# Weight-decode steps and three instruction positions in a spectral layer with two experts

## Chip, core and metric

One core of one Trainium2 chip. The number is the device time of one execution in microseconds; a kernel's time is the median of its runs. TensorE is PE in the profile, with PEld for its weight loads; VectorE is DVE, ScalarE is ACT, GpSimd is POOL, SyncE is SP (here it only issues DMAs).

## What is computed

x is 2 x 3008 x 256, float32. The two experts' weight matrices (256 x 2048 in, 2048 x 256 out) come as float64.

```python
X = np.fft.rfft(x, axis=1)
Yr = Xr @ w_r - Xi @ w_i + b_r
Yi = Xr @ w_i + Xi @ w_r + b_i
Yr, Yi = (np.sign(Y) * np.maximum(np.abs(Y) - 0.01, 0.0) for Y in (Yr, Yi))
x = np.fft.irfft(Yr + 1j * Yi, n=3008, axis=1).reshape(6016, 256)
h = x @ moe_w_in;  x = (h - np.tanh(h)) @ moe_w_out
h = x @ moe2_w_in; out = (h * np.clip(h + 3.0, 0.0, 6.0) / 6.0) @ moe2_w_out
```

## The kernel before

**Precision.** Most products take three matmuls (`three_pass`, L118 to L121): each float32 operand is split into a rounded "hi" part (a copy on ACT into the type fp32r) and a "lo" rest (a subtraction on DVE, sometimes on POOL), and hi x hi, hi x lo and lo x hi are summed.

**Spectral part.** The Fourier transform is split as 47 x 64. `dft_a` (47 points) runs for 8 chunks of the first sequence ahead of the loop and for the 8 chunks of the second inside it, one per iteration for t = 0 to 7; its results are stored to DRAM. The loop over t = 0 to 23 (L659 to L717) takes two frequencies per iteration and is pipelined over four stages: `linear(t)` (24 matmuls), `dft_c(t-2)` (6), `dft_b(t+2)` (8), and `dft_a` (4). `load_bi` brings the stored chunks back, `load_bm` and `load_cm` the transform matrices (`bmt` for `dft_b`). Behind `linear(t)` come on DVE the three instructions of `shrink` (L342 to L344: bias and threshold), then `evict_b_lo` (L315), then `shrink_lo` (L354); on ACT `evict_c` (L372), `evict_b_hi` (L308, L309), `shrink_hi` (L350), `evict_b_neg` (L320). From t = 17 on, `dft_d` and `op_hi`, `op_lo`, `op_sub` make the operands of the first expert pass: sums and differences of input blocks, each split into hi and lo; `op_sub` of T3 and T4 is at L716 and L717, on POOL.

**Experts.** 16 passes k (`NS = 8` per expert) of 2 x 376 tokens, each of 8 groups g of 256 hidden columns. A group (`group`, L563) forms its 2 x 2 block product with seven products instead of eight (p1, p2, p5, p6, p3, p7, p4), applies the nonlinearity `nl`, splits the result (`nl_split`), and, between its products, issues the output products `outp` of the group before it. p1, p6, p7 and p4 of a group go through one PSUM bank `al`: p6 waits for ACT's copy of p1 (L575), p7 for ACT's copy of p6 (L587), p4 for DVE's sum with p7 (L596). The very first group (`first_group`, L532) is a generator whose pieces the loop's end places between the last `dft_c`; its copies of p1, p5 and p6 are L538, L540 and L546, its sums L539, L547 and L552.

**Weight decode.** There is no float64 arithmetic: each of 32 chunks (8 each of 1i and 1o for the first expert, then 8 of 2i, 8 of 2o) is loaded as raw 64-bit words (`w_load`, L156, 512 KB), turned into float32 by bit operations and split. `w_steps` (L162) is a generator; one `w_step()` issues one to three instructions. A chunk of an input matrix takes seven steps, one of an output matrix five: the two ACT conversions (L172, L173); DVE's L175 with ACT's hi copy of the chunk before (L182); DVE's L185, behind which SP is given the next raw load; DVE's lo part of the chunk before (L190); the rounding add (L197); and for input matrices two steps of two short adds (L201 to L205). Three raw buffers exist, so the load issued behind L185 has to wait on SP until that L185 is done, and everything later on SP waits with it. Second-expert chunks are stored to DRAM (`w2id`, `w2od`) and reloaded in passes 7 and 8.

The engines' orders are written out by hand (`manual_schedule`): every engine executes its instructions in the order in which the program issues them. Where decode steps go is said by these lines:

```python
NDEC, NST = 13, 2                                  # L138
for _ in range(2):                                 # L679, and range(NST) at L702
    if t > 1 and ptr["dec"] < NDEC:
        w_step()
if 1 <= g < 6 or k == 0 and g > 0:                 # L770
    if (pos in "bcd" or k == 0) and k < NS:
        w_step()
```

`ptr["dec"]` counts finished chunks; `hook` calls `super_hook` at positions a to e of each group: a comes behind the nonlinearity of p1, b behind p3, c and d around the last output products, e at the group's end. With L785 the first pass also makes sure that a group's weights are decoded before it (it finds them so).

Of the kernel before, what the change touches and what calls it, by code (L numbers as in the profile page):

```python
# [87 lines left out]
def spectral_moe_kernel(ctx: ExitStack, tc: tile.TileContext, x, w_r, w_i, b_r, b_i,  # L88
                        w1i, w1o, w2i, w2o, am, bm, cm, dm, out):
    nc = tc.nc  # L90
    pe, act, dve, pool, sp = nc.tensor, nc.scalar, nc.vector, nc.gpsimd, nc.sync
# [43 lines left out]
        W[nm, c] = pl.tile([128, 2, n], F32R, tag=f"w{kind}{c}", name=f"w{kind}{c}")  # L135
        return W[nm, c]

    NDEC, NST = 13, 2  # L138
    w_src = {"1i": w1i, "1o": w1o, "2i": w2i, "2o": w2o}
    w_order = [(nm, c) for c in range(8) for nm in ("1i", "1o")]  # L140
    w_order += [(nm, c) for nm in ("2i", "2o") for c in range(8)]
# [1 line left out]
    ptr = {"load": 0, "dec": 0}  # L143
# [68 lines left out]
    def w_step():  # L212
        next(w_gen, None)
# [98 lines left out]
    def evict_b_lo(j):  # L312
        pq, h = xf_t[j]
        l = wl.tile([128, 4, 192], F32R, tag="fl", name="fl")
        dve.tensor_tensor(out=l[:, :, 64:192], in0=pq, in1=h.bitcast(F32)[:, :, 64:192], op=ALU.subtract)  # L315
        xf_t[j] = (h, l)
# [5 lines left out]
    def linear(j):  # L322
        h, l = xf_t.pop(j)
        p = bank("acc")
        pv = p.rearrange("p (k d) -> p k d", k=2)
        for k in range(2):
            n = 0
            for dh in range(2):
                q = 2 * k + dh
                for wsel, off in ((0, 64), (1, 0)):  # L330
                    three_pass(pv[:, k, :], h[:, q, off:off + 128], l[:, q, off:off + 128],
                               lwH[:, wsel, dh, :], lwL[:, wsel, dh, :], n == 0, n == 3)
                    n += 1
        s_t[j] = pv
# [13 lines left out]
    def shrink_hi(j):  # L348
        s, sh, sl = s_t[j]
        act.activation(out=sh, in_=s, func=ACTF.Copy)  # L350
# [6 lines left out]
    def dft_c(j):  # L357
        b, kp = divmod(j, K1 // 2)
        sh, sl = s_t.pop(j)
        p = bank("acc")  # L360
        pv = p.rearrange("p (k d) -> p k d", k=2)
        for k in range(2):
            kk = 2 * kp + k
            ch, cl = (v[:, kk * 128:(kk + 1) * 128] for v in (cmH, cmL))
            three_pass(pv[:, k, :], ch, cl, sh[:, k, :], sl[:, k, :], True, True)
        s_t[j] = pv
# [10 lines left out]
    NS = 8  # L377
    xtf = bmt.rearrange("p k f -> p (k f)")[:, 0:4 * NT].rearrange("p (a t) -> p a t", a=4)
    ttf = bmt.rearrange("p k f -> p (k f)")[:, 1536:1536 + 4 * NT].rearrange("p (a t) -> p a t", a=4)
    B11, B12, B21, B22 = (xtf[:, i, :] for i in range(4))  # L380
    T1, T2, T3, T4 = (ttf[:, i, :] for i in range(4))
# [24 lines left out]
    def op_sub(out, a, b, eng=pool):  # L406
        eng.tensor_tensor(out=out, in0=a, in1=b, op=ALU.subtract)  # L407
# [200 lines left out]
    with tc.manual_schedule():  # L608
# [19 lines left out]
        for w in (w_r, w_i):  # L628
            t = wl.tile([128, 2, D], F32, tag="ly", name="lwf")
# [27 lines left out]
        NP = K1  # L657
        a_next = 8
        for t in range(NP):  # L659
            linear(t)  # L660
            if t > 1:
                dft_c(t - 2)
            if t + 2 < NP:
                dft_b(t + 2)
            ab = dft_a(a_next, False) if a_next < 16 else None
            if t > 1:
                evict_c(t - 2)
            if t + 2 < NP:
                evict_b_hi(t + 2)
            shrink(t)  # L670
            shrink_hi(t)
            if t + 2 < NP:
                evict_b_lo(t + 2)
            if t == NP - 1:
                first = first_group()
                next(first)
            if t + 2 < NP:
                evict_b_neg(t + 2)
            for _ in range(2):  # L679
                if t > 1 and ptr["dec"] < NDEC:  # L680
                    w_step()
            shrink_lo(t)
            for nm in {20: ("b11", "b21"), 21: ("t1",), 22: ("t2", "b22")}.get(t, ()):
                op_lo(0, nm)
            if t == 20:
                op_sub(T1, B12, B11, dve)
            if t == 21:
                op_sub(T2, B22, T1, dve)
            if ab:
                dft_a_out(a_next, ab)  # L690
                a_next += 1
            flush_stores()
            if t % 2 == 0:
                load_bm(t // 2 + 2)
                load_cm(t // 2 + 1, s_t[t][0].bitcast(F32)[0:1, 0, 0:1])
            if t > 0:
                load_x(10 + t)
            if t in (0, 1):
                w_load()
            if t % 2 == 1:  # L700
                load_bi((t + 1) // 2 + 2)
            for _ in range(NST):  # L702
                if t > 1 and ptr["dec"] < NDEC:
                    w_step()
            if t == 14:
                load_din(0, din0)
            if t == 15:
                load_din(1, x1[2])
            if t in (17, 18):
                dft_d(0, t - 17, "h")  # L710
            if t in (19, 20):
                dft_d(1, t - 19, "h")
            for nm in {19: ("b11", "b21"), 20: ("t1",), 21: ("t2", "b22")}.get(t, ()):
                op_hi(0, nm)
            if t == 22:
                op_sub(T3, B22, B12)  # L716
                op_sub(T4, B21, T2)  # L717

        next(first)
        dft_c(NP - 2)  # L720
# [12 lines left out]
        def super_hook(k, g, pos):  # L733
# [12 lines left out]
            if n < 2 * NS:  # L746
# [20 lines left out]
                    op_sub(T4, B21, T2)  # L767
                if g == 7 and pos == "e":
                    op_split(n, "b22")
            if 1 <= g < 6 or k == 0 and g > 0:  # L770
                if (pos in "bcd" or k == 0) and k < NS:
                    w_step()
            if pos == "e" and k in (NS - 1, NS):
                if k == NS - 1:
                    w_until(17 + g)
# [52 lines left out]
```

## Time and profile before

| | |
|---|---|
| three runs, median (lowest to highest) | 1226.78 us (1226.3 to 1228.44) |
| the profiled execution | 1225.78 us, of which its span is 1224.0 us |
| PE busy | 1183.5 us, 97% |
| PEld busy | 1163.0 us, 95% |
| DVE busy | 962.5 us, 79% |
| ACT busy | 880.8 us, 72% |
| POOL busy | 158.7 us, 13% |
| DMA | 96.51 MB, 79 GB/s over the span |

The page divides the span into 40 slices; PE is at 90% or more in most of them, below that in the first three, the sixth and the eighth. A share of the whole span says little about one stretch, so the rows below are by stretch. A matmul's row gives its start, its duration and how many were merged; matmuls overlap, so a stretch is measured from start to start.

### The profile page before, as it was taken

What the parts mean: (1) busy time and instruction counts of PE and PEld (TensorE: products, weight loads), DVE (VectorE), ACT (ScalarE), POOL (GpSimd) and SP (SyncE); (2) the same over time, 40 slices, a digit from 0 to 9 for tenths busy, and PEclk for the clock granted to TensorE, in tenths of its full rate; (3) what the DMA queues carried; (4) which work ended last, traced back from release to release, by engine and by line L of the source; (5) the groups of instructions that cost most, each with busy time, mean ns of one, the idle gap of its engine ahead of it and who ended that gap; (6) DMA issues with size and microseconds to landing.
All of it is one profiled execution on the core that took longest, in us unless ns stands there. A gap on an engine that the chain in (4) does not pass through costs nothing.

```text
span 1224.0 us, 20880 instructions
## 1 busy us (share of the span) xinstructions
PE 1183.5 (97%) x7824; PEld 1163.0 (95%) x7824; DVE 962.5 (79%) x1808; ACT 880.8 (72%) x1836; POOL 158.7 (13%) x164
## 2 busy tenths in 40 slices
PE   5899979899999999999999999999999999999998
PEld 3799969899999999999999999999999999999998
DVE  0479988888888888888778787878787878787875
ACT  3477767777787777777777777777777777777775
POOL 1000010201102020202021320202020202020200
PEclk9899989999999999999999999999999999999999
DMA  9896522232212122211104530101010101001000
GB/s 269 239 334 209 185 86 67 99 106 74 74 49 98 66 69 69 61 60 44 43 1 166 185 130 1 51 1 52 1 52 1 52 1 35 18 22 31 10 18 26
DMA packets 47797, 96.51 MB, mean 79 GB/s; under 512 B 4448, under 2 KB 27488, under 8 KB 47696
## 3 DMA queue, kind: packets, MB, share of 16 engines
q1 hardware_dynamic: 41728, 74.08, 18.8%
q0 software_dynamic: 4032, 14.68, 3.9%
q10 hardware_dynamic: 1936, 6.42, 1.4%
q8 instruction: 61, 1.00, 0.3%
q14 instruction: 40, 0.33, 0.1%
HBM read 58.73 MB, written 36.44 MB: 78 GB/s over the span
## 4 chain that ended last, share of the span: by engine, by line
PE 76%; DVE 10%; ACT 10%; issue 3%; DMA 2%; SPq 0%; ACTq 0%; DVEq 0%
PE acc L119 13%; PE acc L121 13%; PE acc L120 13%; PE al L119 7%; PE al L120 6%; PE al L121 6%; PE be L121 3%; PE be L120 3%; PE be L119 3%; ACT gh L115 2%; DVE g L440 2%; PE ga L398 2%; PE ga L120 2%; PE ga L121 2%; PE ga L119 1%
## 5 line engine op out<-in xcount | busy, mean ns | idle before, releaser
L116 DVE TENSOR_TENSOR gl<-g,gh 128x376 fp32r<-128x376 f32 x509 | 290.4, 571 | 149.7 <-ACT gh L115 122.1
L115 ACT ACTIVATE gh<-g 128x376 fp32r<-128x376 f32 x509 | 263.5, 518 | 185.5 <-DVE g L443 91.8
L121 PE MATMUL acc<-wo,gl 128*128 128x256 f32 (+1 forms) x768 | 215.9, 281 | 0.0
L120 PE MATMUL acc<-wo,gh 128*128 128x256 f32 (+1 forms) x768 | 215.8, 281 | 0.0
L119 PE MATMUL acc<-wo,gh 128*128 128x256 f32 (+1 forms) x768 | 215.7, 281 | 0.0
L119 PE MATMUL acc<-gh,wo 128*128 128x376 f32 x512 | 173.2, 338 | 0.0
L121 PE MATMUL acc<-gh,wo 128*128 128x376 f32 x512 | 171.0, 334 | 0.0
L120 PE MATMUL acc<-gl,wo 128*128 128x376 f32 x512 | 170.7, 333 | 0.0
L120 PEld LDWEIGHTS acc<-wo,gh 128*128 128x128 f32 (+1 forms) x768 | 143.0, 186 | 0.0
L121 PEld LDWEIGHTS acc<-wo,gl 128*128 128x128 f32 (+1 forms) x768 | 143.0, 186 | 0.0
L119 PEld LDWEIGHTS acc<-wo,gh 128*128 128x128 f32 (+1 forms) x768 | 142.8, 186 | 0.0
L407 POOL TENSOR_TENSOR bmt<-bmt 128x376 f32<-128x376 f32 x62 | 73.9, 1192 | 521.5 <-ACT bmt L400 396.8
L443 DVE SCALAR_TENSOR_TENSOR g<-e,c 128x376 f32<-128x376 f32 x192 | 119.3, 621 | 12.5 <-ACT e L442 7.9
L442 ACT ACTIVATE e<-c,three 128x376 f32<-128x376 f32 x192 | 116.7, 608 | 8.0 <-DVE c L589 7.2
L440 DVE TENSOR_TENSOR g<-c,e 128x376 f32<-128x376 f32 x189 | 113.9, 603 | 8.2 <-ACT e L439 6.0
L423 POOL TENSOR_TENSOR cmL<-bmt,cmH 128x376 fp32r<-128x376 f32 x60 | 66.1, 1102 | 325.8 <-ACT cmH L418 322.5
L439 ACT ACTIVATE e<-c 128x376 f32<-128x376 f32 x189 | 97.5, 516 | 7.9 <-DVE c L589 7.7
L119 PEld LDWEIGHTS acc<-gh,wo 128*128 128x128 f32 x512 | 96.4, 188 | 0.0
L120 PEld LDWEIGHTS acc<-gl,wo 128*128 128x128 f32 x512 | 96.3, 188 | 0.0
L121 PEld LDWEIGHTS acc<-gh,wo 128*128 128x128 f32 x512 | 96.1, 188 | 0.0
L119 PE MATMUL al<-cmH,wi 128*128 128x376 f32 x256 | 87.8, 343 | 6.3 <-ACT bi_all L538 2.9
L579 ACT ACTIVATE s<-be 128x376 f32<-128x376 f32 x127 | 61.9, 487 | 39.8 <-PE be L121 39.4
(164 smaller groups left out, 2830.8 us busy)
## 6 DMA issues: line engine op xcount, KB each, us to landing
raw<-in_moe_w_in_dram SPq DMA_DIRECT2D x16, 512.0 KB, 5.0
raw<-in_moe_w_out_dram SPq DMA_DIRECT2D x16, 512.0 KB, 4.4
w2id<-wout SPq DMA_DIRECT2D x8, 896.0 KB, 4.3
wi<-w2id POOLq DMA_DIRECT2D x8, 896.0 KB, 4.9
bi_all<-s SPq DMA_DIRECT2D x12, 512.0 KB, 6.5
y1d<-y SPq DMA_DIRECT2D x32, 188.0 KB, 2.0
bmt<-y1d SPq DMA_DIRECT2D x8, 752.0 KB, 4.9
s<-co SPq DMA_DIRECT2D x23, 256.0 KB, 5.5
```

Source lines behind the costliest of these rows:

```text
L115: act.activation(out=hi, in_=src, func=ACTF.Copy)
L116: (lo_eng or dve).tensor_tensor(out=lo, in0=src, in1=hi.bitcast(F32), op=ALU.subtract)
L119: pe.matmul(out=out_ap, lhsT=lh, rhs=rh, start=start, stop=False, **kw)
L120: pe.matmul(out=out_ap, lhsT=lh, rhs=rl, start=False, stop=False, **kw)
L121: pe.matmul(out=out_ap, lhsT=ll, rhs=rh, start=False, stop=stop, **kw)
L407: eng.tensor_tensor(out=out, in0=a, in1=b, op=ALU.subtract)
L423: (eng or dve).tensor_tensor(out=l, in0=OPS[nm][0], in1=h.bitcast(F32), op=ALU.subtract)
L439: act.activation(out=e, in_=src, func=ACTF.Tanh)
L440: dve.tensor_tensor(out=g, in0=src, in1=e, op=ALU.subtract)
L442: act.activation(out=e, in_=src, func=ACTF.Relu, bias=three)
L443: dve.scalar_tensor_tensor(out=g, in0=e, scalar=6.0, in1=src, op0=ALU.min, op1=ALU.mult)
L579: act.activation(out=s5, in_=be, func=ACTF.Copy)
```

## The change

The number of decode steps per loop iteration becomes 6 for t < 10 (three at each place), and 2 plus 1 + t % 2 from t = 10 (it was 4 throughout, from t = 2). The loop decodes the same 13 chunks, in 81 steps: t = 2 to 9 issue 48 of them (32 before), the last stands in t = 19 (t = 22 before). In the experts' first pass steps stand at positions a to d of groups 1 to 5 until 16 chunks are done (17 steps); before, at a to e of groups 1 to 7 (35 steps). The 18 others go to passes 1 to 6, which get position a of groups 1, 3 and 5 beside b, c, d of groups 1 to 5. In the last iteration `shrink_hi` comes behind the first piece of `first_group`. T3 and T4 are subtracted on DVE instead of POOL.

```diff
@@ -135,7 +135,7 @@
-    NDEC, NST = 13, 2
+    NDEC = 13
@@ -668,15 +668,17 @@
             shrink(t)
-            shrink_hi(t)
+            if t < NP - 1:
+                shrink_hi(t)
             if t + 2 < NP:
                 evict_b_lo(t + 2)
             if t == NP - 1:
                 first = first_group()
                 next(first)
+                shrink_hi(t)
             if t + 2 < NP:
                 evict_b_neg(t + 2)
-            for _ in range(2):
+            for _ in range(3 if t < 10 else 2):
                 if t > 1 and ptr["dec"] < NDEC:
                     w_step()
@@ -699,7 +701,7 @@
-            for _ in range(NST):
+            for _ in range(3 if t < 10 else 1 + t % 2):
                 if t > 1 and ptr["dec"] < NDEC:
                     w_step()
@@ -713,8 +715,8 @@
             if t == 22:
-                op_sub(T3, B22, B12)
-                op_sub(T4, B21, T2)
+                op_sub(T3, B22, B12, dve)
+                op_sub(T4, B21, T2, dve)
@@ -767,9 +769,10 @@
-            if 1 <= g < 6 or k == 0 and g > 0:
-                if (pos in "bcd" or k == 0) and k < NS:
-                    w_step()
+            if 1 <= g < 6 and k < NS:
+                if pos in "bcd" or pos == "a" and (k == 0 or g % 2):
+                    if k or ptr["dec"] < 16:
+                        w_step()
```

SP's queue in the loop, iterations t = 3 (its end) to t = 5, before. `raw` is a raw weight load, `s_0` a store of `dft_c`'s result, `bmt` a transform table, `xb` a chunk of x, `bi_all` a reload for `dft_b`:

```order
L254 DMA xb_100<-in_x_dram 14x1024
L290 DMA bi_all<-s_0_60 128x4x256
L156 DMA raw<-in_moe_w_in_dram 128x2x256
L259 DMA s_0_62<-co 128x2x256
L613 DMA bmt<-in_bm_dram 128x512
L254 DMA xb_98<-in_x_dram 80x1024
L254 DMA xb_98<-in_x_dram 14x1024
L156 DMA raw<-in_moe_w_out_dram 128x2x256
```

And the same place in the changed kernel:

```order
L290 DMA bi_all<-s_0_60 128x4x256
L156 DMA raw<-in_moe_w_out_dram 128x2x256
L259 DMA s_0_62<-co 128x2x256
L613 DMA bmt<-in_bm_dram 128x512
L254 DMA xb_98<-in_x_dram 80x1024
L254 DMA xb_98<-in_x_dram 14x1024
L156 DMA raw<-in_moe_w_in_dram 128x2x256
```

The raw load of iteration 3 has gone ahead of `xb_100` and `bi_all`, and the `bmt` load of iteration 4 now stands behind a raw load of its own iteration; the same holds in iteration 6.

ACT at the end of the loop (from the last `evict_b_neg`) and in the first pieces of `first_group`, before:

```order
L320 ACTIVATE fl<-fl 128x4x64
L172 ACTIVATE ws<-raw 128x512
L173 ACTIVATE ws<-raw 128x512
L182 ACTIVATE wi_1763<-ws 128x896
L418 ACTIVATE cmH<-bmt 128x376
L418 ACTIVATE b22h<-bmt 128x376
L372 ACTIVATE co<-acc 128x512
L350 ACTIVATE sh<-ly 128x512
L372 ACTIVATE co<-acc 128x512
L350 ACTIVATE sh<-ly 128x512
L538 ACTIVATE bi_all<-al 128x376
L540 ACTIVATE bi_all<-be 128x376
```

And in the changed kernel:

```order
L320 ACTIVATE fl<-fl 128x4x64
L418 ACTIVATE cmH<-bmt 128x376
L418 ACTIVATE b22h<-bmt 128x376
L372 ACTIVATE co<-acc 128x512
L350 ACTIVATE sh<-ly 128x512
L372 ACTIVATE co<-acc 128x512
L538 ACTIVATE bi_all<-al 128x376
L540 ACTIVATE bi_all<-be 128x376
L350 ACTIVATE sh<-ly 128x512
```

The three decode instructions are gone from there, and L538 and L540 stand ahead of the last L350.

DVE in group 7 of the first pass, from its L577 on, before:

```order
L116 TENSOR_TENSOR gl<-g,gh 128x376
L440 TENSOR_TENSOR g<-c_2616,e 128x376
L190 TENSOR_TENSOR wout<-ws,wout 128x896
L589 TENSOR_TENSOR c_2647<-be,su 128x376
L116 TENSOR_TENSOR gl<-g,gh 128x376
L197 ISA ws<-ws 128x1024
L440 TENSOR_TENSOR g<-c_2647,e 128x376
L596 TENSOR_TENSOR c_2670<-al,s_2618 128x376
```

And in the changed kernel:

```order
L116 TENSOR_TENSOR gl<-g,gh 128x376
L440 TENSOR_TENSOR g<-c_2586,e 128x376
L589 TENSOR_TENSOR c_2615<-be,su 128x376
L116 TENSOR_TENSOR gl<-g,gh 128x376
L440 TENSOR_TENSOR g<-c_2615,e 128x376
L596 TENSOR_TENSOR c_2637<-al,s_2588 128x376
```

Only the group's own instructions are left there.

## Rows read from the trace of the kernel before

**Rows 1.** Busy time by stretch: bounds, length, busy us (instructions) by engine, PE clock, DMA.
```profile
42.00:159.60 117.60, 116.08 (x929) 111.80 (x927) 100.91 (x182) 82.92 (x163) 7.80 (x16) 1.00 0.71 227
159.60:180.10 20.50, 13.17 (x65) 11.66 (x64) 17.68 (x34) 11.50 (x24) 1.05 (x1) 0.83 0.32 101
180.10:256.40 76.30, 69.63 (x395) 66.50 (x394) 66.41 (x131) 56.77 (x121) 11.40 (x9) 0.98 0.27 83
256.40:1224.00 967.60, 961.42 (x6340) 954.85 (x6339) 774.76 (x1459) 715.64 (x1504) 134.15 (x128) 1.00 0.16 52
```

**Rows 2.** Who PE waited for, 42 to 180 us: total, times, longest.
```profile
PE al L119 <- ACT bi_all L538: 2.9, 1, 2.9
PE acc L121 <- DVE fl L315: 2.0, 2, 1.5
...
PE al L119 <- DVE bi_all L552: 0.7, 1, 0.7
```

**Rows 3.** The same, 180 to 257 us, the two largest.
```profile
PE al L119 <- DVE c L596: 2.9, 2, 2.3
PE al L119 <- ACT su L587: 2.0, 3, 0.9
```

**Rows 4.** PE, instructions in time (start, us): last `dft_b`; group 1 of the first pass.
```profile
154.70 1.05 PE L301 MATMUL ga<-bmt,bi_all 128*128 128x128 f32 x8
...
180.12 0.33 PE L119 MATMUL al<-cmH,wi 128*128 128x376 f32 x1
```

**Rows 5.** PE: p1 of group 7, then of pass 1's groups 0 and 1.
```profile
247.30 0.52 PE L119 MATMUL al<-cmH,wi 128*128 128x376 f32 x1
...
256.38 0.34 PE L119 MATMUL al<-cmH,wi 128*128 128x376 f32 x1
...
264.11 0.34 PE L119 MATMUL al<-cmH,wi 128*128 128x376 f32 x1
```

**Rows 6.** Chain of waits, pieces in time: first `dft_d` of passes 1 and 2.
```profile
270.46 0.86 PE ga L398 x8
...
336.52 0.86 PE ga L398 x8
```

**Rows 7.** PE: `dft_b` of t = 6 and 7, then of t = 9 and 10.
```profile
79.67 1.05 PE L301 MATMUL al<-bmt,bi_all 128*128 128x128 f32 x8
85.85 1.05 PE L301 MATMUL ga<-bmt,bi_all 128*128 128x128 f32 x8
...
96.46 1.05 PE L301 MATMUL ga<-bmt,bi_all 128*128 128x128 f32 x8
100.90 1.05 PE L301 MATMUL al<-bmt,bi_all 128*128 128x128 f32 x8
```

**Rows 8.** DVE in time: one loop iteration's start, and that three later.
```profile
102.18 0.67 DVE L342 TENSOR_TENSOR ly<-acc,bias 128x512 f32<-128x512 f32 x1
...
104.56 1.08 DVE L190 TENSOR_TENSOR wi<-ws,wi 128x896 fp32r<-128x896 f32 x1
...
106.16 0.69 DVE L354 TENSOR_TENSOR sl<-ly,sh 128x512 fp32r<-128x512 f32 x1
...
117.07 0.68 DVE L342 TENSOR_TENSOR ly<-acc,bias 128x512 f32<-128x512 f32 x1
```

**Rows 9.** SP and DVE in iteration 4, and the landing times of all `bmt` loads.
```profile
68.53 0.52 SPq L613 DMA_DIRECT2D bmt<-in_bm_dram  x1
...
69.59 1.08 DVE L190 TENSOR_TENSOR wi<-ws,wi 128x896 fp32r<-128x896 f32 x1
...
DMA to landing us min/median/max: 5.7/7.2/9.1
```

**Rows 10.** DMA rate in 40 slices of 50 to 100 us.
```profile
GB/s 10 88 266 318 374 351 252 234 105 349 368 398 281 330 342 360 360 397 371 380 352 226 56 221 428 400 231 279 396 395 379 405 343 244 13 71 331 147 206 345
```

**Rows 11.** T4's subtraction on POOL, and DVE beside it.
```profile
165.71 1.05 POOL L407 TENSOR_TENSOR bmt<-bmt 128x376 f32<-128x376 f32 x1 [7.03 <-issue]
...
165.94 1.36 DVE L185 SCALAR_TENSOR_TENSOR ws<-ws,raw 128x512 uint32<-128x512 uint32 x1
```

## The prediction

> **What bounds the kernel now.** The page first: PE is busy 97% of the span, so time can be won only where PE stands still or runs at a low clock. The table by stretches shows where that is [rows 1]. From 256 us to the end PE is busy 961.4 of 967.6 us at full clock; nothing is to be had there. In the loop, 42 to 159.6 us, it is idle for 117.6 - 116.1 = 1.5 us. The two stretches between are different. From 159.6 to 180.1 us, the loop's last two iterations and the first group, PE works 13.2 of 20.5 us, and at a mean clock of 0.83. From 180.1 to 256.4 us, the experts' first pass, it works 69.6 of 76.3 us.
>
> Then the list of PE's waits for these two. At the loop's end it waits 2.9 us for ACT's copy of p1 and 2.0 us for DVE's L315 [rows 2]; in the first pass 2.9 us for DVE's third sum and 2.0 us for ACT's copy of p6 [rows 3]. Neither engine is slow in these instructions; they come late because decode steps stand ahead of them in the same queues. So the bound in both stretches is the order on DVE and ACT.
>
> How much is there? At the loop's end, from the last `dft_b` to group 1 is 180.12 - 154.70 = 25.4 us [rows 4]. PE's own work in that stretch: one iteration without `dft_a` takes 100.90 - 96.46 = 4.44 us [rows 7]; the next one lacks `dft_b`, 0.9 us, so 3.55; two more `dft_c` at 6/38 of an iteration, 0.7 each, 1.4; and the first group's 21 matmuls. A group without `dft_d` takes 264.11 - 256.38 = 7.73 us for its 45 matmuls [rows 5], 0.172 us each, so 3.6. Sum 13.0 us: at most 12.4 us can be won. In the first pass, the seven groups with decode and the group behind them take 256.38 - 180.12 = 76.3 us [rows 4, 5]; eight groups of a later pass, `dft_d` included, 336.52 - 270.46 = 66.1 us [rows 6]. At most 10.2 us can be won.
>
> **The change, part by part.**
>
> Front of the loop, t = 2 to 9, 16 more steps. DVE sets their price. Behind L342 it takes 104.56 - 102.18 = 2.38 us for four of an iteration's five own instructions, and L354 0.69: 3.07 [rows 8]. Three iterations with 12 steps take 117.07 - 102.18 = 14.89 us, so a step costs (14.89 - 9.21)/12 = 0.47 us. Six steps make 3.07 + 2.84 = 5.9 us. PE needs 85.85 - 79.67 = 6.18 us as long as `dft_a` runs (to t = 7), so DVE's addition is hidden there. In t = 8 and 9 PE needs 4.44: DVE falls behind by 2.9 us; from t = 10 to 18 at 3.5 steps it needs 4.73, another 2.6 us. Before, at 4 steps (4.96), it fell behind by 4.7 us in t = 8 to 16, and PE lost less than 1.5 us by it [rows 1]. With up to 5.5 us PE may lose a little more or a little less: zero, with -0.8 and +1.5 as ends. From t = 17 on the queue drains, since `dft_d` lengthens PE's iterations and the steps end in t = 19.
>
> SP and DMA in the front. Two of the moved steps count here, since they carry a raw load ahead of a `bmt` load, in t = 4 and t = 6. Before, the `bmt` load of t = 4 was issued at 68.53; PE needed it at 79.67 (`dft_b` of t = 6), 11.1 us later [rows 7, 9]. Now SP first waits for the L185 that frees the raw buffer. It stands where DVE's L190 stood at 69.59, so it ends at about 70.3, and with two issues ahead `bmt` goes out at about 71.1: 8.6 us are left. Landing took 5.7, 7.2 or 9.1 us (least, median, most) [rows 9], and the 0.5 MB put ahead costs 1.2 us at the highest rate seen, 428 GB/s, 1.8 us at 285 GB/s, the mean of the 40 slices [rows 10]. At the median nothing or 0.4 us is late; at the worst 2.3 us; and the same once more for t = 6. From 0 to +4.6 us; I take +1.0, near the median.
> The Trainium skill (DMA: Bandwidth & Descriptors, Specifications) gives a core 358 GB/s of HBM bandwidth, which would leave no room in the 14 of 40 slices that are at or above that and so speaks against putting loads here. The trace disagrees: slices reach 428 GB/s [rows 10]. By the page's figure 0.5 MB would take 1.5 us, an estimate, between my two.
>
> End of the loop. No steps stand in t = 20 to 22, so DVE and ACT come to the last iteration without a backlog, the waits for L315 go [rows 2], and the clock should stay up. L538 and L540 ahead of the last L350 take away the 2.9 us for p1's copy. What stays is a chain: last `linear`, `shrink` and split, last `dft_c`; and in the first group p7 behind the copy of p6, p4 behind L552, for which PE waits 0.7 us as before [rows 2]. I put 16.9 us in place of 25.4: PE's 13.0, the 0.7, and about 3 us for the split, for p7, and for p1's own lateness, of the size of the waits that remain. That is -8.5; ends -12.4 (PE's work alone) and -2.9 (the copy alone).
>
> T3 and T4 on DVE. Beside T4 on POOL, an L185 took 1.36 us instead of the 0.69 of a 512-wide DVE instruction such as L354 [rows 8, 11]. So POOL's two cost DVE about 1.3 us; on DVE itself they are narrower than L354, so at most 0.69 each, 1.4. Zero; it stands where DVE has no backlog any more.
>
> First pass, 35 steps to 17. Groups 6 and 7 have none, as in a later pass; group 5 one; groups 1 to 4 four each instead of five. Of the 10.2 us I leave 1.3, for those four groups: -8.9. Ends 0 and -10.2.
>
> Passes 1 to 6, 18 more steps. They add 18 x 0.47 = 8.5 us to DVE, which there is busy 774.8 of 967.6 us [rows 1], and stand beside PE's work. Each odd group has a step ahead of the copy of p6 that frees PE's p7; that can cost a few tenths where the step has ACT instructions (5 of 16). +0.5. If DVE's slack were gone there, every step would cost; that is a rival below. The weights are stored and reloaded a pass or more later, so their stores stay hidden.
>
> Sum against the profiled execution: 1225.78 + 0 + 1.0 - 8.5 + 0 - 8.9 + 0.5 = 1209.9 us. It stands 1.0 us under the median of the runs, 1226.78, so the prediction is **1210.9 us**, 15.9 us or 1.3% less.
>
> **The rivals.**
>
> *The front pays for the loads.* Both `bmt` loads land at their worst, 4.6 us instead of 1.0: 1214.5 us. For it: 8.6 us are left against 7.2 to 9.1. Against: the second load has the first one's delay as slack.
>
> *Only the copy is won at the loop's end.* The 25.4 us there are a chain of dependences rather than a backlog, and -2.9 stands in place of -8.5: 1216.5 us. For it: DVE also has the operands of pass 0 to make there. Against: PE's wait for L315 and the decode rows in both queues.
>
> *Slower: groups of four steps are bound by DVE and ACT in the later passes.* There are 16 of these (groups 1, 3, 5 of passes 1 to 5, group 1 of pass 6). With about five steps the seven groups of the first pass took 247.30 - 180.12 = 67.2 us [rows 4, 5] for some 58.3 of PE's work (66.1 less 7.73), 1.27 us each too long. If four steps cost as much, 16 x 1.27 = 20.3 us replace the 0.5, and 1210.9 becomes 1230.7 us, slower than before. It decides from (1226.78 x 1.002 - 1210.4)/16 = 1.18 us a group. For it: ACT and DVE wait for each other within a group, so a busy share under 100% doesn't prove room. Against: groups with three steps cost PE nothing, and groups 6, 7 and 0 of each pass, without steps, let a backlog drain.
>
> *No change that can be told.* The copy alone at the loop's end, and half of that price in the later passes: 1216.5 + 10 = 1226 us.
>
> That fewer steps are moved than meant is excluded: they are counted in the engines' orders.
>
> **How the numbers follow.** My forecast 0.60, the front 0.14, the copy alone 0.12, slower 0.07, no change 0.07. Measurements of this kernel tell about 0.2% (2.5 us) from no change, so the chances are faster 0.86, within 0.2% 0.07, slower 0.07. The range runs from 1205, where nearly all of PE's idle time is won (1226.78 - 12.4 - 10.2 + 1 = 1205.2), to 1218, which takes in the front and the copy alone, and leaves the last two cases out and little more.
>
> **What the changed profile would show.** Right: `dft_b` of the last iteration still near 155 us; group 1 at about 172 instead of 180 us, pass 1's group 1 near 240; PE's waits in the first pass under 2 us; no wait for L538 behind L350; PE still without waits from there to the end. The front is wrong if PE waits for `bmt` or `bi_all` by more than 1 us. The forecast as a whole would be wrong if passes 1 to 6 took more than 66.1 us each, or if DVE still trailed PE by several microseconds in t = 22.

## Result and the profile after

The changed kernel takes 1214.7 us, median of four runs (1214.16 to 1216.59); on the same chip the kernel before took 1226.54 us. The ratio is 0.9909, interval 0.9894 to 0.9924. The forecast was 1210.9 us and the range 1205 to 1218. The profiled execution took 1214.16 us with a span of 1212.4 us, against 1225.78 and 1224.0 us before. The page's first line, and from its 40 slices those of PE and its clock:

```profile
PE 1180.3 (97%) x7824; PEld 1160.4 (96%) x7824; DVE 959.2 (79%) x1810; ACT 880.7 (73%) x1836; POOL 158.1 (13%) x162
...
PE   5899989999999999999999999999999999999998
...
PEclk8899999999999999999999999999999999999999
```

The shares have hardly moved; 12 us of 1224 don't show there. The comparison has to be by stretch, and each stretch must begin and end at the same matmul in both kernels. I take the start of `dft_b` in iterations 1, 8, 16 and 21 (the last one), then of the second product in group 1 of the first pass, then of the second product in group 1 of pass 1, then the end. Busy time by stretch, columns as in [rows 1]; the kernel before, cut at these points:

```profile
47.56:92.02 44.46, 43.65 (x325) 40.53 (x323) 33.73 (x60) 31.70 (x62) 3.58 (x9) 1.00 0.93 305
92.02:128.04 36.02, 35.92 (x306) 35.68 (x305) 34.64 (x65) 25.24 (x51) 1.23 (x3) 1.00 0.61 186
128.04:154.70 26.66, 26.14 (x225) 25.90 (x223) 25.09 (x46) 20.81 (x41) 0.00 (x0) 1.00 0.63 198
154.70:180.64 25.94, 18.52 (x106) 16.72 (x105) 22.40 (x40) 14.31 (x31) 2.42 (x2) 0.87 0.31 91
180.64:256.90 76.26, 69.59 (x393) 66.46 (x393) 66.37 (x130) 56.74 (x121) 11.40 (x9) 0.98 0.27 84
256.90:1224.00 967.10, 960.92 (x6337) 954.35 (x6336) 774.35 (x1458) 715.14 (x1503) 134.15 (x128) 1.00 0.16 52
```

The changed kernel:

```profile
45.93:92.23 46.30, 44.10 (x324) 40.64 (x323) 38.10 (x70) 34.45 (x67) 3.96 (x9) 1.00 0.96 296
92.23:130.89 38.66, 36.99 (x307) 36.06 (x306) 36.59 (x71) 25.53 (x52) 1.54 (x3) 1.00 0.72 229
130.89:157.60 26.71, 26.36 (x225) 26.05 (x223) 23.98 (x43) 20.62 (x42) 0.00 (x0) 1.00 0.50 156
157.60:176.72 19.12, 15.83 (x106) 14.47 (x105) 16.77 (x32) 11.78 (x25) 0.28 (x1) 0.94 0.19 63
176.72:243.21 66.49, 66.36 (x394) 65.76 (x393) 56.27 (x108) 51.76 (x111) 9.56 (x9) 0.99 0.17 52
243.21:1212.40 969.19, 961.92 (x6337) 953.83 (x6336) 781.59 (x1480) 719.71 (x1512) 136.81 (x128) 1.00 0.16 55
```

Read the length (the number behind the bounds) and DVE's busy time (the third busy figure, behind PE's and PEld's) against each other:

| stretch | length | difference | DVE's work, difference | forecast |
|---|---|---|---|---|
| ahead of t = 1 | 47.56 to 45.93 | -1.6 | not changed | 0 |
| front, t = 1 to 8 | 44.46 to 46.30 | +1.8 | +4.4 | +1.0 |
| middle, t = 8 to 16 | 36.02 to 38.66 | +2.6 | +2.0 | 0 |
| t = 16 to 21 | 26.66 to 26.71 | +0.1 | -1.1 | 0 |
| end of the loop | 25.94 to 19.12 | -6.8 | -5.6 | -8.5 |
| first pass | 76.26 to 66.49 | -9.8 | -10.1 | -8.9 |
| later passes | 967.10 to 969.19 | +2.1 | +7.2 | +0.5 |
| span | 1224.0 to 1212.4 | -11.6 | | -15.9 |

So the changed kernel did not lose decode work; it holds it elsewhere. DVE's 10.1 us taken out of the first pass gave 9.8; 7.2 us of it went to the later passes and cost 2.1. In the loop it is a poor trade: what the end gained the front and the middle lost, but for 2.3 us. The -1.6 ahead of the loop belongs to no part of the change: over all the profiles of this study that stretch lies between 45.2 and 48.5 us, also where the code is the old one.

Not all of the gain is idle time. In the first pass PE's idle time falls from 6.7 to 0.1 us, and its busy time for as many matmuls from 69.59 to 66.36. At the loop's end idle time falls from 7.4 to 3.3 us and busy time from 18.52 to 15.83, at a granted clock of 0.94 instead of 0.87. Cut at the first product of the first group, the end shows where that is; before, then changed:

```profile
154.70:168.61 13.91, 10.49 (x70) 9.82 (x69) 13.04 (x24) 8.29 (x17) 2.42 (x2) 0.88 0.27 76
168.61:180.64 12.03, 8.03 (x38) 6.90 (x37) 9.36 (x17) 6.02 (x14) 0.00 (x0) 0.86 0.35 109
...
157.60:165.59 7.99, 7.99 (x70) 7.99 (x69) 7.42 (x14) 5.27 (x11) 0.00 (x0) 1.00 0.14 49
165.59:176.72 11.13, 7.84 (x38) 6.48 (x37) 9.35 (x18) 6.51 (x15) 0.28 (x1) 0.89 0.22 73
```

Ahead of that product 5.9 us are won: PE no longer stands still there, and its granted clock is 1.00 instead of 0.88. Behind it, it is 0.9 us.

PE's instructions in time: `dft_b` of t = 21, then the first product of group 1, then that of pass 1's group 1 (the counterparts of [rows 4, 5], whose products at 247.30, 256.38 and 264.11 us are those of pass 1's groups 0, 1 and 2; the prediction's sums use them so):

```profile
157.60 1.05 PE L301 MATMUL ga<-bmt,bi_all 128*128 128x128 f32 x8
...
175.78 0.52 PE L119 MATMUL al<-cmH,wi 128*128 128x376 f32 x1
...
242.69 0.33 PE L119 MATMUL al<-cmH,wi 128*128 128x376 f32 x1
```

By the first products, as the prediction counted, the end takes 18.2 us (25.4 before) and the first pass 66.9 (76.3). The product at 175.78 takes 0.52 us and the later one 0.33: from 174.5 to 177.7 us the granted clock is 0.50, the lower of its two levels (1.2 of 2.4 GHz), after PE had been busy for only 5.7 of the 8.9 us from 165.6 to 174.5.

Who PE waited for, 40 to 180 us (total, times, longest; the four largest), the counterpart of [rows 2]:

```profile
PE acc L121 <- DVE fl L315: 2.0, 4, 0.8
PE acc L119 <- ACT sh L350: 2.0, 1, 2.0
PE al L301 <- ACT wo L182: 1.3, 1, 1.3
PE al L119 <- DVE bi_all L552: 0.7, 1, 0.7
```

The 2.9 us for L538 are gone, but 2.0 us for the last L350 stand there now. The four waits for L315 all lie in the loop, ahead of 160 us; the kernel before has one there, of 0.5 us. From 180 to 250 us, where [rows 3] had 2.9 and 2.0 us, PE has no wait at all. From 250 us to the end, where it had none before, it has these:

```profile
PE al L119 <- ACT s L575: 0.8, 3, 0.4
PE al L119 <- ACT su L587: 0.2, 1, 0.2
PE al L119 <- DVE c L596: 0.2, 1, 0.2
```

### The profile page after: what moved, and what is told of

Read it like the earlier page. It is cut to its first block, busy times and chain, and to the rows that moved or that the text cites. A ratio compares the mean times of both kernels' runs of the same rounds, so it can differ in the third digit from the quotient of the medians.

```text
span 1212.4 us, 20876 instructions
## 1 busy us (share of the span) xinstructions
PE 1180.3 (97%) x7824; PEld 1160.4 (96%) x7824; DVE 959.2 (79%) x1810; ACT 880.7 (73%) x1836; POOL 158.1 (13%) x162
## 4 chain that ended last, share of the span: by engine, by line
PE 73%; ACT 11%; DVE 11%; issue 3%; DMA 2%; ACTq 0%; SPq 0%; DVEq 0%
PE acc L121 12%; PE acc L119 12%; PE acc L120 12%; PE al L119 7%; PE al L120 6%; PE al L121 6%; PE be L121 3%; PE be L120 3%; PE be L119 3%; ACT gh L115 3%; DVE g L440 2%; PE ga L398 2%; DVE gl L116 2%; PE ga L121 2%; PE ga L120 2%
## 5 line engine op out<-in xcount | busy, mean ns | idle before, releaser
L407 POOL TENSOR_TENSOR bmt<-bmt 128x376 f32<-128x376 f32 x60 | 73.8, 1230 | 448.0 <-ACT bmt L400 332.1
```

## Experiments

Four kernels do one part of the change alone, on the kernel before; the next six alter one thing in the changed kernel, and the last two several. "Front", "middle", "end", "first pass" and "rest" are the stretches of the table. Ratios are to the kernel before on the same chip.

**Only the steps inside the loop.**

```diff
-            for _ in range(2):
+            for _ in range(3 if t < 10 else 2):
...
-            for _ in range(NST):
+            for _ in range(3 if t < 10 else 1 + t % 2):
```

> The kernel before with the change's numbers of decode steps in the loop alone. If the stages are independent (my account): the loop from t = 1 to the last dft_b takes about 111.7 us instead of 107.1, the end of the loop loses its backlog but keeps PE's wait for the copy of p1 behind the last L350, so some 20.5 to 21 us instead of 25.4; the first pass stays near 76 us; the whole -0.5 to +1 us against before. Rival (the loop's end is won by the missing backlog alone, the copies' place is idle): the end takes about 18 us, the whole -2.5 us.

Measured: 1225.25 against 1225.39 us, ratio 0.9995 (0.9983 to 1.0007). Front 46.20, middle 38.65, end 20.15, first pass 76.15, rest 966.77. The largest of PE's waits from 46 to 182 us:

```profile
PE al L119 <- ACT bi_all L538: 3.0, 1, 3.0
```

And from 178 to 257 us:

```profile
PE al L119 <- DVE c L596: 2.9, 2, 2.4
PE al L119 <- ACT su L587: 2.0, 3, 0.9
PE al L119 <- ACT s L575: 1.7, 3, 0.8
```

The loop to t = 21 loses 4.5 us and its end wins 5.8; on the whole that is nothing that can be told. The first pass keeps its length and its waits, although it now begins with less backlog from the loop: its loss was made by its own steps, as the next run confirms.

**Only the steps of the passes.**

```diff
-            if 1 <= g < 6 or k == 0 and g > 0:
-                if (pos in "bcd" or k == 0) and k < NS:
-                    w_step()
+            if 1 <= g < 6 and k < NS:
+                if pos in "bcd" or pos == "a" and (k == 0 or g % 2):
+                    if k or ptr["dec"] < 16:
+                        w_step()
```

> The kernel before with the change's places of decode steps in the experts' passes alone. My account: groups 1 to 7 of the first pass and the group behind them take about 67 us instead of 76.3, passes 1 to 6 about 1.9 us more, loop and its end as before: -7.4 us. Rival (the first pass is long because it inherits the loop's backlog): less than half of the 9.4 us in the first pass, so -2 to -3 us.

Measured: 1216.4 us, ratio 0.9922 (0.9907 to 0.9937). Loop (t = 1 to 21) and end as before (107.24 and 26.00), first pass 66.61, rest 968.90. Busy time of 180 to 256.4 us, the stretch in which PE had worked 69.63 of 76.30 us [rows 1]:

```profile
180.00:256.40 76.40, 76.14 (x451) 75.03 (x450) 66.14 (x130) 60.51 (x130) 9.23 (x9) 1.00 0.18 56
```

PE now works through. This part alone gives 0.78% of the whole change's 0.91%, and the intervals of the two overlap.

**Only the copies ahead of the last rounding.**

```diff
-            shrink_hi(t)
+            if t < NP - 1:
+                shrink_hi(t)
...
                 next(first)
+                shrink_hi(t)
```

> The kernel before with the last L350 behind the copies of p1 and p5 alone. My account: PE's 2.9 us wait for L538 goes, but the last dft_c then waits for L350 and L354 behind DVE's backlog as in the changed kernel (2.0 us there), so the loop's end takes 1 to 3 us less: -1 to -3 us. Rival (the copies' place alone is what the loop's end gains): -5 us or more there.

Measured: ratio 0.9994 (0.9984 to 1.0003), end 25.60 us, 0.3 less than before, where 1 to 3 were expected. The wait for L538 is gone from PE's list, and this one is new:

```profile
PE acc L119 <- ACT sh L350: 1.4, 1, 1.4
```

The last `dft_c` now waits for the rounding that was put back. The end again, cut at the first product of the first group:

```profile
152.49:167.20 14.71, 11.26 (x71) 10.61 (x69) 13.82 (x25) 8.56 (x18) 2.43 (x2) 0.77 0.28 79
167.20:178.09 10.89, 8.37 (x39) 6.78 (x37) 9.06 (x17) 6.54 (x15) 0.29 (x1) 0.79 0.32 112
```

Behind that product, where the copies stand, the end is 1.1 us shorter (10.89 against 12.03); ahead of it, where nothing was moved, this profile loses 0.8, at a granted clock of 0.77 instead of 0.88. So the 0.3 us are a sum of two things, and the copies are worth about 1 us (the three profiles with the old counts in the loop and the old place of the copies lie between 12.03 and 12.31). That is still less than half of the wait's 2.9: DVE's chain to the last `dft_c` has the same backlog ahead of it.

**Only T3 and T4 on DVE.**

```diff
-                op_sub(T3, B22, B12)
-                op_sub(T4, B21, T2)
+                op_sub(T3, B22, B12, dve)
+                op_sub(T4, B21, T2, dve)
```

> The kernel before with T3 and T4 subtracted on DVE alone. My account: DVE loses 0.92 us to two own instructions and gets back the 1.3 us for which its instructions were held beside POOL's, so the loop's end changes by -0.5 to +0.5 us. Rival (both stand in DVE's queue ahead of the last shrink and are paid on the path): +0.9 us at the loop's end.

Measured: ratio 0.9996 (0.9987 to 1.0005), end 25.42 us: no change. The Trainium skill (Perfetto Trace Analysis, Optimizing Scalar/DVE Operations) says that moving work between DVE and GpSimd may not help, since they share a read port; the run agrees for this direction of the move. The L185 that took 1.36 us beside POOL's T4 [rows 11] takes 0.69 here, which pays for most of the 0.9 us that the two subtractions take on DVE. In this profile the middle took 37.96 us instead of 36.02, with the loop's code unchanged there. A single profile's stretch can be off by this much, so what follows rests on stretches that recur: the middle is 36.01 or 36.02 us in three profiles with the old counts (before, the passes alone, the copies alone), and 38.60 to 38.66 in four with the new ones (39.06 in a fifth, the next run, with another wait in it).

**Raw loads of t = 3 to 6 behind the reload for `dft_b`.** In the changed kernel, `w_load` in these iterations is only counted, and issued behind `load_bi`, so that no `bmt` load stands behind one.

```diff
-                w_load()
+                if ptr.get("defer"):
+                    ptr["pending"] = ptr.get("pending", 0) + 1
+                else:
+                    w_load()
...
+            ptr["defer"] = t in (3, 4, 5, 6)
...
+            w_load(ptr.pop("pending", 0))
+            ptr["defer"] = False
             for _ in range(3 if t < 10 else 1 + t % 2):
```

The trace of the changed kernel gave the reason. SP's issues in iteration 4:

```profile
68.85 0.39 SPq L156 DMA_DIRECT2D raw<-in_moe_w_out_dram  x1
69.33 0.53 SPq L259 DMA_DIRECT2D s<-co  x1
70.15 0.35 SPq L613 DMA_DIRECT2D bmt<-in_bm_dram  x1
```

What SP waited for from 60 to 72 us, the largest (total, times, longest):

```profile
SPq L156 <- DVE ws L185: 5.0, 2, 3.2
```

And PE's `dft_b` of t = 6:

```profile
79.23 1.13 PE L301 MATMUL al<-bmt,bi_all 128*128 128x128 f32 x8 [1.27 <-ACT wo L182]
```

The trace puts the 1.27 us down to ACT's L182, which has no part in `dft_b`. It needs two loads, `bi_all` and `bmt`. The `bi_all` load of iteration 3 was issued at 64.81 us, and none of them took over 7.7 us to land. The `bmt` load of 70.15 took this long:

```profile
DMA to landing us min/median/max: 9.0/9.0/9.0
```

70.15 + 9.0 is 79.15, so it was `bmt`; the same load had landed after 5.7 us in the kernel before. PE would have been there at 79.23 - 1.27 = 77.96 us, 7.8 us after the issue, where before it had 11.1 us [rows 7, 9]. SP had spent the time on the raw load (L156) ahead of it, waiting for L185. In the kernel before SP waits as long for L185 between 60 and 72 us (5.3 us, one wait), but behind that `bmt` load.

> The changed kernel with the raw weight loads of t = 3 to 6 issued on SP behind the same iteration's loads of bmt, x and dft_b's input. If the front's loss is the late bmt load (my account): PE's wait of 1.3 us ahead of dft_b of t = 6 goes and t = 3 to 7 take about 1.5 to 2 us less. Rival (the DMA engines are full there, whatever the order): t = 3 to 7 change by less than 0.5 us. Rival two: the loss comes back later as more DVE backlog, since DVE rather than PE sets the pace, and the whole stays the same.

Measured: ratio 0.9907 (0.9889 to 0.9926). The front falls to 43.90 us, below that of the kernel before; the middle is 39.06, the end 19.12. PE's waits for loads, 40 to 180 us:

```profile
PE al L304 <- DMA bi_all<-s: 2.2, 1, 2.2
...
PE al L304 <- DMA bmt<-in_bm_dram: 0.4, 1, 0.4
```

So the order of the loads does set the front's loss: DVE is busy there for 37.98 us, as in the changed kernel (38.10), and the steps alone cost nothing. `dft_b` of t = 10 now waits 2.2 us for its reload, but the middle is only 0.4 us longer for it: PE's waits for the instruction that is L315 in the changed kernel fall from 2.0 to 1.0 us. From t = 1 to group 1 this kernel takes 128.79 us, the changed one 130.79. In this profile the first pass takes 67.91 us instead of 66.49, with PE busy throughout in both and a granted clock of 0.97 instead of 0.99. That the loop gains 2.0 us rests on one profile; the whole does not show it.

**All steps of t >= 10 at the second place.**

```diff
-            for _ in range(3 if t < 10 else 2):
+            for _ in range(3 if t < 10 else 0):
...
-            for _ in range(3 if t < 10 else 1 + t % 2):
+            for _ in range(3 if t < 10 else 3 + t % 2):
```

> The changed kernel with all steps from t = 10 on at the second place (behind shrink_lo), the same number per iteration. If the middle of the loop loses time because a step's DVE part stands right behind its ACT conversions, which stand behind the last L350 (DVE idle 1.0 us for them in t = 13 and 15): those idle times go, the middle (t = 8 to 18) loses about 2 us instead of 4.1, the whole is 1 to 2 us faster. Rival (the sheer number of steps makes the backlog): the middle still loses 3.5 to 4 us.

Measured: 1217.39 us, ratio 0.9939 (0.9918 to 0.9961). The middle stays at 38.78 us; DVE's two idle times of 1.0 us ahead of L175 (waiting for ACT's L172) are gone, and nothing comes of it. So their place does not make the middle's loss; the rival, their number, is left. The front took 47.47 us with equal code there; that accounts for part of the kernel's being slower than the changed one by the medians (the intervals overlap), the rest stays open.

**Six steps only for t < 8, then four.**

```diff
-            for _ in range(3 if t < 10 else 2):
+            for _ in range(3 if t < 8 else 2):
...
-            for _ in range(3 if t < 10 else 1 + t % 2):
+            for _ in range(3 if t < 8 else 2):
```

> The changed kernel with six steps only up to t = 7 and four from t = 8. If the backlog is made by six-step iterations without dft_a beside them (t = 8 and 9, 2.9 us): the middle loses 2 to 3 us instead of 4.1, as in the kernel before (1.4) with a little more, and the loop's end is the same or a little longer. Rival (the number of steps from t = 8 to 19 is what counts, and it is nearly the same): no change in the sum of middle and end.

Measured: ratio 0.9915 (0.9898 to 0.9931). The middle falls from 38.66 to 37.40 us, half of the way back; end 19.03, first pass 67.08. Fewer steps in t = 8 and 9 shorten the middle, where DVE was busy for 36.59 of 38.66 us (here 35.58). This is one profile, and the whole does not show it.

**No step at position a in the later passes.**

```diff
-                if pos in "bcd" or pos == "a" and (k == 0 or g % 2):
+                if pos in "bcd" or pos == "a" and k == 0:
```

> The changed kernel without position a in passes 1 and later (three steps per group, the last chunks in pass 7). If the 1.9 us that passes 1 to 6 take more are the fourth steps: passes 1 to 6 go back to 396.5 us from 398.4, pass 7 stays within 0.3 us: -1.5 to -2 us. Rival (they come from which instructions fall together at positions c and d, not from the number): passes 1 to 6 stay within 0.5 us of 398.4.

Measured: ratio 0.9919 (0.9899 to 0.9939), rest 968.89 us instead of 969.19. Passes 1 to 6 (from the second product of one's group 0 to the next's) take 397.4 us together, the changed kernel's 398.4, those before 396.5; but the steps left over go into pass 7, which takes 63.53 us instead of 62.46. Of the four groups that the changed kernel lengthens most, two recur without position a: group 2 of pass 3 takes 9.15 us (9.05; 8.64 before), group 1 of pass 4 8.13 (8.17; 7.74 before). These are not made by the fourth step of a group. The two largest losses, 0.5 us each in group 6 of pass 3 and group 1 of pass 5, do not recur, and 1.1 us are lost in group 2 of pass 7 instead.

**T3 and T4 behind the last `shrink`.**

```diff
                 next(first)
                 shrink_hi(t)
...
+            if t == NP - 1:
+                op_sub(T3, B22, B12, dve)
+                op_sub(T4, B21, T2, dve)
...
-            if t == 22:
-                op_sub(T3, B22, B12, dve)
-                op_sub(T4, B21, T2, dve)
```

The reason is DVE's queue at the loop's end in the changed kernel, from the lo parts of two operands on:

```profile
166.53 0.55 DVE L423 TENSOR_TENSOR cmL<-bmt,cmH 128x376 fp32r<-128x376 f32 x1
166.99 0.54 DVE L423 TENSOR_TENSOR b22l<-bmt,b22h 128x376 fp32r<-128x376 f32 x1
167.45 1.00 DVE L407 TENSOR_TENSOR bmt<-bmt 128x376 f32<-128x376 f32 x2
168.37 0.68 DVE L342 TENSOR_TENSOR ly<-acc,bias 128x512 f32<-128x512 f32 x1
```

And ACT's beside it:

```profile
166.33 0.48 ACT L538 ACTIVATE bi_all<-al 128x376 f32<-128x376 f32 x1
167.34 0.49 ACT L540 ACTIVATE bi_all<-be 128x376 f32<-128x376 f32 x1 [0.53 <-PE be L121]
170.34 0.63 ACT L350 ACTIVATE sh<-ly 128x512 fp32r<-128x512 f32 x1 [2.51 <-DVE ly L344]
```

ACT is idle for 2.5 us ahead of the last L350. DVE comes late to the last `shrink`, and 1.0 us of that are T3 and T4 (L407).

> The changed kernel with T3 and T4 (still on DVE) behind the last shrink_lo instead of ahead of the last shrink. If the loop's end is a DVE queue in which everything ahead of the last shrink counts: the last shrink starts 0.92 us sooner and the end (last dft_b to group 1's p2) takes 0.5 to 1 us less than 19.1. Rival (p7 waits for T3's split instead): no change, or up to 0.5 us more.

Measured: ratio 0.9913 (0.99 to 0.9925), end 19.35 us. PE's waits at the loop's end:

```profile
PE acc L119 <- ACT sh L350: 1.1, 1, 1.1
...
PE al L120 <- DVE t3l L423: 0.8, 1, 0.8
```

The wait for L350 falls from 2.0 to 1.1 us, and p7 waits 0.8 us for the lo part of T3, which now comes later. DVE has this work to do either way.

**Nine chunks in the loop instead of thirteen.**

```diff
-    NDEC = 13
+    NDEC = 9
```

> The changed kernel with the loop decoding 9 chunks instead of 13, so that no step stands in t = 13 to 23; the first pass has to decode the rest, some ahead of its groups. If what is left at the loop's end is still decode backlog: the middle loses under 2 us instead of 4 (t = 8 to 16 in under 37.5 us) and the end takes about 17 us instead of 19.1. Rival (the end is now a chain of the last iterations' own instructions): the end takes 18.5 us or more. The first pass pays: some 26 steps more, at about 0.5 us each where groups can't hide them, so 5 to 12 us more there, and the whole is slower than the changed kernel.

Measured: 1222.74 us, ratio 0.9976 (0.9965 to 0.9986). Busy time of the middle and of the end:

```profile
93.03:129.82 36.79, 36.59 (x306) 35.89 (x305) 35.28 (x65) 25.25 (x51) 1.54 (x3) 1.00 0.74 236
...
155.60:173.15 17.55, 15.81 (x106) 14.46 (x105) 14.58 (x28) 10.72 (x23) 0.29 (x1) 0.94 0.18 61
```

With no step left in the loop's second half, the middle is 1.9 us shorter than in the changed kernel and the end 1.6 us; the front, with the same steps, stays at 46.18. The 17.55 us are what the end takes without any decode backlog; the changed kernel is 1.6 above it. No decode step of DVE's runs there in either; what differs is how far DVE is in its queue, for its last `shrink` (L342) starts 9.2 us after the last `dft_b` here and 10.8 us after it in the changed kernel. The four chunks come back in the first pass, which takes 79.23 us, 12.7 more than in the changed kernel where 5 to 12 were expected.

**Two attempts at a faster version.** The first takes the deferred loads (t = 3 to 7), six steps for t < 8, then two and 1 + t % 2, and T3 and T4 behind the last `shrink`:

```diff
+            ptr["defer"] = 3 <= t <= 7
...
-            for _ in range(3 if t < 10 else 2):
+            for _ in range(3 if t < 8 else 2):
...
-            for _ in range(3 if t < 10 else 1 + t % 2):
+            for _ in range(3 if t < 8 else 1 + t % 2):
```

> The changed kernel with three edits together: raw loads of t = 3 to 7 behind the iteration's other loads, six steps only up to t = 7 (then 2 plus 1 + t % 2), T3 and T4 behind the last shrink_lo. If the three losses are independent: front 43.9 us instead of 46.3, middle about 37 instead of 38.7, no or a shorter wait for bi_all at t = 10 than the 2.2 us of the kernel with the loads moved up to t = 6 (the raw load of t = 7 now also stands behind it), end 18.5 instead of 19.1: 3 to 5 us faster than the changed kernel. Rival (DVE's total sets the loop): under 1.5 us faster, since what the front wins the middle waits for.

The second also leaves one chunk more to the first pass:

```diff
-    NDEC = 13
+    NDEC = 12
...
-            if 1 <= g < 6 and k < NS:
+            if 1 <= g < 6 + (k == 0) and k < NS:
```

> The same with 12 chunks decoded in the loop instead of 13, and steps in group 6 of the first pass too. If the middle's loss is the number of steps there: 1 to 2 us less in the loop and its end, and nothing in the first pass, whose group 6 has room: 1 to 2 us faster than the kernel with the three edits. Rival: the first pass takes as much more as the loop takes less.

Measured: 1215.7 us, 0.9919 (0.9905 to 0.9933), and 1214.04 us, 0.9904 (0.989 to 0.9917). Neither can be told from the changed kernel's 0.9909; the 3 to 5 us expected of the first did not come. The front is 45.30 and 45.83 us, but the middle 40.15 and 40.26, the longest of the study; the first one's end is 21.44 (its last step stands in t = 20, the changed kernel's in t = 19), the second one's 17.27, and the second one's first pass 69.70. In the first one's middle, DVE, 90 to 140 us, has a wait that the changed kernel does not have:

```profile
DVE fl L318 <- ACT fh L312: 3.1, 1, 3.1
```

DVE is busy for only 34.21 of these 40.15 us: that points to a late operand, and not to DVE's sum. The second attempt has the same wait. ACT's copy for L318 came late because ACT's `evict_c` ahead of it started at 106.69 us, after 3.0 us of idle time, though the matmuls that it evicts had started by 102.6. What is left for it to wait for is its output buffer `co`, of which there are two: SP issued their stores only at 98.3 to 100.0 us, having issued nothing from 88.6 to 96.8. When these stores landed is not recorded, so this cause is likely, not shown.

## Why the prediction was right in the whole, and where its terms were off

Sign and range held; the forecast was 3.8 us low on the median, 4.3 on the profiled execution. By its steps:

- **First pass, -8.9:** -9.8 measured (-9.4 by the first products, as the prediction counted). Shown: the passes alone give -9.7 here and almost the whole gain, PE's waits are gone, and the loop alone leaves the first pass at 76.15 us. The 1.3 us kept back for groups 1 to 4 were too much by 0.9 (0.5 by the first products).
- **End of the loop, -8.5:** -6.8 (-7.2 by the first products). The mechanism holds: the loop's counts alone give -5.8, and the clock stays up ahead of the first group, as the prediction said. The size failed in "DVE and ACT come to the last iteration without a backlog". The run with nine chunks shows 17.55 us without one, near the 16.9 forecast (which counts to the first product, 0.5 to 0.9 us earlier); the 1.6 us above it are DVE's work left over from t = 19 and before (six profiles with 13 chunks in the loop and the other two parts of the change take 19.0 to 19.8 us there).
- **The copies:** not priced alone in the sum. Alone they end the wait for L538 and win 0.3 us over the end, within the scatter of a stretch, and 1.1 behind the first group's first product, where the scatter is smaller. The bound -2.9 "the copy alone" took the wait's length for its worth, which the experiment speaks against: the last `dft_c` waited behind the same backlog.
- **T3 and T4, 0:** no change, as forecast; the place mattered as little.
- **Middle of the loop, "zero, with -0.8 and +1.5 as ends":** +2.6, outside both ends. This is the step that failed most. I had put the backlog of 5.5 us beside the 4.7 before and taken PE's loss to be like before's. But DVE was already busy for 34.64 of 36.02 us in this stretch; that left 1.4 us of room for 2.0 us more of work, and PE's waits for L315 in the loop grew from 0.5 to 2.0 us. The run with all steps at the second place (38.78) speaks against their place; the runs with fewer steps in t = 8 and 9 (37.40) and with none late (36.79) speak for their number, with one profile each, in a stretch where one profile was 1.9 us off with unchanged code.
- **Front, +1.0 for the `bmt` loads:** +1.8, within 0 to +4.6. Only one of the two loads made PE wait by more than 1 us. It took 9.0 us to land: that is the prediction's median with its price for the load put ahead (7.2 + 1.8), not its worst case (9.1 + 1.8). The step that was off is the slack: of the 11.1 us from issue to need 7.8 were left, where I had put 8.6. Behind it stands SP's wait for L185. The Trainium skill (DMA: Bandwidth & Descriptors, Anatomy of one DMA — SWDGE (gpsimd) path, in a note on the DMA engines) says that a wait on a semaphore happens on the issuing sequencer before the transfer is handed on, not on the DMA engines; the trace agrees, with SP's 5.0 us of such waits from 60 to 72 us, and every later load stood behind them. They are no longer than before (5.3 us); new is that this `bmt` load stands behind one. Of the 1.8 us, 1.4 stand between `dft_b` of t = 5 and that of t = 6, where the wait of 1.3 us is; t = 4 and 6 lose 1.0 more, t = 3 wins 0.6 (before, a wait of 0.7 us for `bmt` stood there), and these are not assigned.
- **Passes 1 to 6, +0.5:** +2.1 from pass 1 to the end. The slower rival's 1.27 us for each of 16 groups fell: the whole is about 0.1 us for each. The waits of 1.2 us in all, for L575, L587 and L596, are the kind the prediction named; the other 0.9 us show no wait, but PE's busy time there is 1.0 us longer for as many matmuls (961.92 against 960.92 us), which also stays open. The run without position a only moved the loss (1.0 us less in passes 1 to 6, 1.1 more in pass 7), so the term's reason, "a step ahead of the copy of p6", is not shown; what makes the single long groups stays open.
- **The signs that the prediction named:** PE waits neither for L538 nor at all in the first pass, as said, but it does wait behind the first pass (1.2 us). The three products come 2.6 to 3.8 us later than said (157.6, 175.8 and 242.7 us). "PE waits for `bmt` or `bi_all` by more than 1 us" came, with 1.3: by its own sign the prediction was wrong on the front. Passes 1 to 6 at "more than 66.1 us each" came too, but narrowly: five of the six take 66.2 to 67.0 us, and in the kernel before they take 66.0 to 66.4, so the sign was set too close to tell anything.

The errors partly cancelled: 0.8 (front), 2.7 (t = 8 to 21), 1.7 (end) and 1.6 (passes) too low, 0.9 (first pass) and 1.6 (the unrelated start) too high, 4.3 in all; that the forecast came so near owes something to this. For the expected gain in the loop the answer is: it was real at the end, and given back ahead of it, in the middle because DVE bounds that stretch too, in the front by the order of the loads.

What stays open: the loop's part together (counts, copies and T3, T4) is worth 0.9922 - 0.9909, 0.13% or 1.6 us by the medians, less than the intervals can tell; the stretches say 2.5 us (133.24 to 130.79 from t = 1 to group 1, the passes alone against the whole change).

## What to carry to other kernels

Price a moved piece of work by the engine that bounds the stretch it leaves and the one it enters: out of DVE's 66 us in a stretch of 76, each microsecond gave nearly one back; into a stretch where DVE was busy for 96% it cost more than one; into one where PE works through and DVE is busy for 80% it cost 0.3. A wait that ends last is worth its length only if the next one in line is not fed by the same backlog; removing 2.9 us of one gave about 1. When work is moved on a queue, look at the loads it carries, and at what they are put ahead of.

## What was not expected of the hardware

A wait that the trace puts down to an engine can be a load's: 1.27 us "for ACT's L182" were `bmt`, landing 9.0 us after its issue. An instruction on DVE took 1.36 us beside a subtraction on POOL and 0.69 us in the same place without it. And the same code took 45.2 to 48.5 us from the program's start to t = 1, and 36.0 or 38.0 us in the middle, in single profiles of kernels that differ only elsewhere; a difference under 2 us in one stretch is therefore weak evidence where a single profile has it, as with the middle of the loop in the kernels with nine chunks and with six steps up to t = 7.
